# Last two token tiles of a linear-attention and feed-forward kernel: matmul order of the plain products, and which engine makes three of the row sums

## The chip, the core and the metric

The kernel runs on one core of one Trainium2 chip. The metric is the device time of one execution in microseconds (us). In the text, TensorE (PE in the profile) does the matmuls, VectorE (DVE) and ScalarE (ACT) the elementwise work, GpSimd (POOL) some elementwise work and the weight loads, SyncE (SP) issues most transfers. A name with a q behind it (SPq, ACTq) is an engine's queue issuing a transfer.

## The reference

```python
# q, k, v: (8 batches, 8 heads, 576 positions, 64); w_in: (512, 2048); w_out: (2048, 512)
q_s = softmax(q, axis=-1)                 # over the 64 features
k_s = softmax(k, axis=2)                  # over the 576 positions
kv  = einsum('bhsd,bhse->bhde', k_s, v)
x   = einsum('bhsd,bhde->bhse', q_s, kv)  # then laid out as (4608 tokens, 512)
h   = x @ w_in
out = maximum(0.01 * h, h) @ w_out        # float32, (4608, 512)
```

## The kernel before

The 4608 tokens are nine tiles of 512. Attention fills `xT` (features on the partitions, bfloat16) batch by batch, and beside it the feed-forward part runs over the tiles: layer 1 writes a 128x512 block of the hidden layer for each of 16 blocks, a leaky ReLU (line 572) takes it out of PSUM, layer 2 (line 584) sums over the 16 blocks. Every engine runs its instructions in the order in which the kernel's text issues them; there is no scheduler behind it. What an engine waits for is put in as semaphore waits.

The last two tiles, number 7 (`TA`, here called tile A) and number 8 (`TB`, tile B), are done otherwise: both layers use a scheme with seven products in place of eight, in which sums of operands are multiplied and the results are added up.

In layer 1 the operands are the two tiles. `pair_layer1(i)` runs for i = 0 to 7 and gives four hidden blocks each time: of tile A, `g7[i]` and `g7[8+i]`, and of tile B, `g8(i)` and `g8(8+i)`. The additions out of PSUM are VectorE's (line 1027), the leaky ReLUs ScalarE's (line 572). The last leaky of tile A, of `u4` into `g7[15]`, is held back to the end.

In layer 2 each tile is cut by token rows into two halves of 256 (h = 0, 1), by the hidden dimension into two halves of 8 blocks (fh = 0, 1), and by output columns into two halves of 256. Written h0(0) for rows half 0, hidden half 0, and so on, a tile needs these operands:

- plain: h0(0) and h0(1), straight from the hidden blocks (products p1, p2)
- row sums, in a 4-byte format for the fast fp32 matmul: r1 = h1(0) + h1(1), r2 = r1 - h0(0), r3 = h0(0) - h1(0), r4 = h0(1) - r2, and c22, a copy of h1(1)
- weight sums v1 to v4 and o22, made long before

A product is `product2`, 16 matmuls of 256 columns: for each of two groups of 128 rows (i), the 8 hidden blocks (m) are summed in PSUM. p5 = r1 v1, p6 = r2 v2, p7 = r3 v3, p4 = c22 v4, p3 = r4 o22. p1, p2, p5, p6, p7 have both row groups in one PSUM bank; p4 and p3 take a bank for each group. There are six such banks, and a product takes the one whose last reader stands earliest in the order; it waits for that reader, an addition.

The order written out at the end of the kernel is, for TensorE: p1 of A, p1 of B, p2 of A, p2 of B, then p5, p6, p7, p4, p3 of A, then p5, p6, p7, p4, p3 of B. For VectorE after the last pair: r2 of A; the output additions of p2 of A (`second`); r4 of A; `second` of B; r1 of B; u2 and u4 (`sixth`); r2 of B; u3 and two output additions (`seventh`); r3 of B; the additions of p4 and p3 (`fourth`, `third`); r4 of B; then `sixth`, `seventh`, `fourth`, `third` of B. The row sums of A are made in parts of 2, 4 and 2 blocks (the blocks lie in different buffers), those of B in two parts of 4 blocks (128x1024).

r1 and r3 of A are made ahead: `sums_ahead(n)`, n = 0 to 3, makes parts of two blocks (128x512) on GpSimd while the pairs run, n = 3 after the last pair. r2 of A is written over nothing, but r1, r2, r3, r4, c22 of B reuse the buffers of A's (r1 of B has one of its own, that of an earlier weight sum), so a sum of B waits for the product of A that reads the same buffer.

Three waits matter later and stand in the built program both before and after the change, beside those for operands: p5 of B takes the bank of p7 of A and so waits for u3 of A on VectorE; r3 of B waits for the last matmul of p7 of A, whose operand it overwrites; p3 of B waits for r4 of B.

An output row group goes out as two transfers (`put`), for tile A both from SyncE's queue, for tile B one from SyncE's and one from ScalarE's.

Of the kernel before, what the change touches and what calls it, by code (L numbers as in the profile page):

```python
# [12 lines left out]
ALU = mybir.AluOpType  # L13
# [13 lines left out]
def kernel(  # L27
# [9 lines left out]
    nc = tc.nc  # L37
# [10 lines left out]
    P = 128  # L48
# [730 lines left out]
    NH = NF // 2  # L779
    CL, CR = slice(0, 2), slice(2, 4)  # L780
    XA, XB = slice(TA * TT, TB * TT), slice(TB * TT, NT * TT)
    late = {}
# [194 lines left out]
    def g7_blocks(h):  # L977
        ts = lambda t: slice(t * TT + h * M2, t * TT + (h + 1) * M2)
        return (
            (slice(0, 2), lambda fh: g7_pairs[fh][:, :, ts(0)]),  # L980
            (slice(2, 4), lambda fh: xT[:, 0:2, ts(4 + fh)]),
            (slice(4, 6), lambda fh: xT[:, 2:4, ts(4 + fh)]),
            (slice(6, 8), lambda fh: xT[:, 2 * fh : 2 * fh + 2, ts(6)]),
        )
# [6 lines left out]
    def g8_wide(h):  # L991
        ts = lambda t: slice(t * TT + h * M2, t * TT + (h + 1) * M2)
        return tuple((slice(4 * b, 4 * b + 4), lambda fh, b=b: xT[:, :, ts(2 * fh + b)]) for b in range(2))

    def late_rows(name, n, pool):
        late[name] = pool.tile([P, NH, M2], F32R, name=n)

    def sums_ahead(n):
        if n == 0:
            for name in ("r3", "r1"):  # L1000
                late_rows(name, name, late["ahead"])
        (ms, h0), (_, h1) = g7_blocks(0)[n], g7_blocks(1)[n]
        for name, x, y, op in (("r3", h0(0), h1(0), ALU.subtract), ("r1", h1(0), h1(1), ALU.add)):
            nc.gpsimd.tensor_tensor(out=late[name][:, ms], in0=x, in1=y, op=op)

    def product(w, a):
        ps = psB_pool.tile([P, TT], FP32, name="pp", tag=BANK_TAG)
# [12 lines left out]
    def pair_layer1(i):  # L1020
# [36 lines left out]
        if i in (2, 4, 6):  # L1057
            sums_ahead(i // 2 - 1)
# [15 lines left out]
    held_leaky[0]()  # L1074
    next(fill, None)
    sums_ahead(3)
    pairs.close()
    last_pool = ctx.enter_context(tc.tile_pool(name="late3", bufs=1, reuse_waits="tile"))

    def product2(a, w, each=False):  # L1080
        if each:
            ps = [psB_pool.tile([P, H2], FP32, name="pq", tag=BANK_TAG) for _ in range(2)]
        else:
            both = psB_pool.tile([P, 2, H2], FP32, name="pq", tag=BANK_TAG)
            ps = [both[:, 0], both[:, 1]]
        for i in range(2):
            for m in range(NH):
                nc.tensor.matmul(  # L1088
                    ps[i],
                    lhsT=a(m)[:, i * P : (i + 1) * P],  # L1090
                    rhs=w(m),
                    start=(m == 0 and (each or i == 0)),
                    stop=(m == NH - 1 and (each or i == 1)),
                )
        return ps if each else both

    def add(o, ps, e):
        nc.vector.tensor_tensor(out=o, in0=ps, in1=e, op=ALU.add)

    def row_sums(wide, name, n, pool, op, x, y):  # L1100
        late_rows(name, n, pool)
        for (ms, h0), (_, h1) in zip(wide(0), wide(1)):
            view = lambda s: late[s][:, ms].bitcast(FP32) if isinstance(s, str) else (h0, h1)[s[0]](s[1])
            o = late[name][:, ms]
            if op is None:
                nc.scalar.copy(out=o, in_=view(x))
            else:
                nc.vector.tensor_tensor(out=o, in0=view(x), in1=view(y), op=op)

    rows = lambda n: (lambda m: late[n][:, m])  # L1110
    plain_g = lambda g, fh: (lambda m: g(fh * NH + m)[:, 0:M2])
    plain_w = lambda fh: (lambda m: w_out_sb[:, fh * NH + m, E1])
    last_adds = lambda n: [last_pool.tile([P, O], FP32, name=f"{n}{i}") for i in range(2)]
    gu = lambda: g_pool.tile([P, 2, H2], FP32, name="gu", tag="gj")
    A = dict(t=TA, o1=[osb_pool.tile([P, O], FP32, name="out_sb") for _ in range(2)], issue=(nc.sync, nc.sync))
    B8 = dict(t=TB, o1=last_adds("o1"), issue=(nc.sync, nc.scalar))
# [6 lines left out]
    def first_two(z):  # L1123
        z["e1"] = gu()
        nc.scalar.copy(out=z["e1"], in_=z["p1"])

    def second(z):
        for i in range(2):
            add(z["o1"][i][:, E1], z["p2"][:, i], z["e1"][:, i])
            put(z, z["o1"][i], 0, i, E1)  # L1130
# [11 lines left out]
    def fourth(z):  # L1142
        for i in range(2):
            add(z["o2"][i][:, E1], z["p4"][i], z["u3"][:, i])
            put(z, z["o2"][i], 1, i, slice(0, O))
# [5 lines left out]

    ga, gb = (lambda n: g7[n]), g8
    ahead_pool = late["ahead"]
    A["p1"] = product2(plain_g(ga, 0), plain_w(0))
    first_two(A)
    row_sums(g7_wide, "r2", "r2", last_pool, ALU.subtract, "r1", (0, 0))
    B8["p1"] = product2(plain_g(gb, 0), plain_w(0))
    first_two(B8)
    row_sums(g7_wide, "c22", "c22", last_pool, None, (1, 1), None)
    A["p2"] = product2(plain_g(ga, 1), plain_w(1))  # L1160
    second(A)
    row_sums(g7_wide, "r4", "r4", last_pool, ALU.subtract, (0, 1), "r2")
    B8["p2"] = product2(plain_g(gb, 1), plain_w(1))
    second(B8)
    A["p5"] = product2(rows("r1"), rows("v1"))
    late["r1"] = strip("r1").rearrange("p a b -> p (a b)")[:, 0 : NH * M2].rearrange("p (m t) -> p m t", t=M2)
    for (ms, h0), (_, h1) in zip(g8_wide(0), g8_wide(1)):
        nc.vector.tensor_tensor(out=late["r1"][:, ms], in0=h1(0), in1=h1(1), op=ALU.add)
    A["p6"] = product2(rows("r2"), rows("v2"))
    A["o2"] = [osb_pool.tile([P, O], FP32, name="out_sb") for _ in range(2)]  # L1170
    B8["o2"] = last_adds("o2")
# [4 lines left out]
    A["p4"] = product2(rows("c22"), rows("v4"), True)  # L1176
    row_sums(g8_wide, "c22", "c22", last_pool, None, (1, 1), None)
    A["p3"] = product2(rows("r4"), rows("o22"), True)
    row_sums(g8_wide, "r3", "r3", ahead_pool, ALU.subtract, (0, 0), (1, 0))
    fourth(A)  # L1180
    third(A)
    B8["p5"] = product2(rows("r1"), rows("v1"))
# [40 lines left out]
```

## Time and profile before

| what | value |
|---|---|
| time, median of 3 runs | 281.03 us (281.0 to 281.08) |
| the profiled execution's own time | 280.83 us |
| its span, first to last instruction | 279.0 us |
| granted TensorE clock, mean | 0.998 |
| TensorE matmul busy | 270.0 us, 97% of the span |
| VectorE busy | 229.2 us, 82% |
| ScalarE busy | 166.1 us, 60% |
| GpSimd busy | 84.2 us, 30% |

Rows of the timeline read: start in us, duration in us, engine, line of the kernel, operation, output and inputs, shapes, x count, and in brackets how long the engine was idle before and what ended that. Neighbouring rows of one kind are merged, and their durations overlap a little because the engines pipeline. Rows of the waits read: engine and line that waited, on whom, then us in total, times, and the longest in us. Rows of the groups read: line, engine, operation, shapes, count, busy us, mean ns of one, and idle us before. Line numbers are those of the kernel before.

### The profile page before, as it was taken

The numbers are of one execution on the slowest core, as the hardware profiler recorded it, in microseconds if no ns is written. First come the engines' busy times: TensorE is split into PE (matmuls) and PEld (weight loads), VectorE is DVE, ScalarE is ACT, GpSimd is POOL, SyncE is SP. The second block draws the span as 40 slices with busy tenths as digits, with TensorE's granted clock in tenths as the row PEclk, the third lists the DMA queues.
The fourth block names the chain that finished last, engine by engine and source line by source line (L and its number), as shares of the span: only waits on it lengthen the run. The fifth ranks groups of instructions, "written<-read, shape, count | busy, mean of one in ns | idle before, by whom it ended". The sixth has DMA issues, their size and how long they took to land.

```text
span 279.0 us, 5241 instructions
## 1 busy us (share of the span) xinstructions
PE 270.0 (97%) x2018; PEld 148.7 (53%) x2018; DVE 229.2 (82%) x327; ACT 166.1 (60%) x291; POOL 84.2 (30%) x105
## 2 busy tenths in 40 slices
PE   8799999999999999999999999999999999999992
PEld 3378644444444544445444544444445566569992
DVE  2996986899999949956795598958959999998993
ACT  3977573783488467754586448664673667673200
POOL 2867460159003004000300085003000898822000
PEclk9999999999999999999999999999999999999999
DMA  7999999987996697099409940430701010111134
GB/s 244 330 208 324 242 254 284 395 261 223 261 391 215 95 392 261 2 224 390 133 0 248 396 101 2 85 77 1 161 0 40 0 38 0 41 38 41 36 87 141
DMA packets 40488, 46.48 MB, mean 167 GB/s; under 512 B 18832, under 2 KB 24208, under 8 KB 40464
## 3 DMA queue, kind: packets, MB, share of 16 engines
q1 hardware_dynamic: 36480, 41.43, 49.3%
q0 software_dynamic: 3504, 4.20, 8.6%
q10 hardware_dynamic: 480, 0.52, 0.6%
q8 instruction: 16, 0.26, 0.4%
q14 instruction: 8, 0.07, 0.1%
HBM read 36.70 MB, written 9.44 MB: 165 GB/s over the span
## 4 chain that ended last, share of the span: by engine, by line
PE 88%; DVE 6%; DMA 2%; issue 1%; ACT 0%; SPq 0%; DVEq 0%
PE ph L563 35%; PE pout L584 34%; PE pq L1088 9%; PE pp L1009 7%; DVE u L1027 3%; DMA k_raw<-in_k_dram 2%; PE po L479 2%; DVE t L160 1%; PE pokv L341 1%; PE pkv L341 1%; DVE c L1027 1%; PE pkv L419 0%; DVE k_raw L410 0%; ACT ke L206 0%; ACT xT L572 0%
## 5 line engine op out<-in xcount | busy, mean ns | idle before, releaser
L584 PE MATMUL pout<-w_out_sb,gj 128*128 128x512 bf16 x448 | 103.7, 380 | 0.0
L563 PE MATMUL ph<-xT,w_in_sb 128*128 128x512 bf16 (+1 forms) x512 | 98.7, 352 | 0.0
L563 PEld LDWEIGHTS <-w_in_sb 128*128 128x128 bf16 x512 | 49.8, 98 | 47.0 <-issue 0.2
L572 ACT ACTIVATE gj<-ph 128x512 bf16<-128x512 f32 x112 | 63.4, 602 | 18.8 <-PE ph L563 18.5
L584 PEld LDWEIGHTS <-gj 128*128 128x128 bf16 x448 | 41.9, 98 | 51.9 <-issue 4.6
L218 POOL CAST vb<-v_raw 128x1152 bf16<-128x1152 f32 x13 | 19.6, 1536 | 83.7 <-DMA v_raw<-in_v_dram 43.6
L578 ACT COPY out_sb<-pout 128x512 f32<-128x512 f32 x24 | 14.0, 584 | 34.1 <-PE pout L584 20.3
L321 DVE TENSOR_REDUCE qsum<-qe 128x36 f32<-128x2304 bf16 (+5 forms) x13 | 20.1, 1543 | 6.3 <-ACT qe L312 6.2
L1027 DVE TENSOR_TENSOR u<-pp,u 128x512 f32<-128x512 f32 x32 | 21.3, 687 | 2.0 <-PE pp L1009 0.5
L206 ACT ACTIVATE ke<-k_raw 128x2304 bf16<-128x2304 f32 (+2 forms) x13 | 18.0, 1383 | 8.2 <-DVE k_raw L198 7.8
L328 DVE TENSOR_TENSOR qe<-qe,qrec 128x2304 bf16<-128x2304 bf16 (+5 forms) x13 | 21.5, 1657 | 0.4
L245 DVE TENSOR_REDUCE qmax<-q_raw 128x36 f32<-128x2304 f32 (+5 forms) x13 | 20.0, 1537 | 0.6 <-DMA q_raw<-in_q_dram 0.6
L312 ACT ACTIVATE qe<-q_raw 128x2304 bf16<-128x2304 f32 (+5 forms) x13 | 17.2, 1322 | 4.2 <-POOL q_raw L304 3.2
L198 DVE TENSOR_TENSOR k_raw<-k_raw,kall 128x1152 f32<-128x1152 f32 (+2 forms) x10 | 18.1, 1821 | 0.3
L304 POOL TENSOR_TENSOR q_raw<-q_raw,qmax 128x512 f32<-128x512 f32 (+3 forms) x7 | 11.8, 1681 | 21.0 <-DVE qmax L245 20.7
L1009 PE MATMUL pp<-s,t 128*128 128x512 f32 x48 | 17.0, 458 | 0.0
L160 DVE TENSOR_TENSOR t<-t 128x256 f32<-128x256 f32 (+2 forms) x22 | 14.4, 654 | 0.7
L361 DVE RECIPROCAL krec<-pokv 128x2 f32<-128x2 f32 x8 | 1.3, 165 | 16.6 <-PE pokv L479 16.6
L500 ACT CAST xT<-po 128x448 bf16<-128x448 f32 (+3 forms) x31 | 13.3, 513 | 1.1 <-PE po L479 1.1
L304 DVE TENSOR_TENSOR q_raw<-q_raw,qmax 128x2304 f32<-128x2304 f32 (+1 forms) x6 | 13.2, 2202 | 0.2
L160 DVE TENSOR_TENSOR t<-k_raw 128x512 f32<-128x512 f32 (+1 forms) x11 | 11.2, 1016 | 1.1 <-DMA k_raw<-in_k_dram 1.0
L1088 PE MATMUL pq<-v,r 128*128 128x256 f32 x96 | 11.9, 284 | 0.0
(122 smaller groups left out, 324.9 us busy)
## 6 DMA issues: line engine op xcount, KB each, us to landing
out_dram<-out_sb SPq DMA_DIRECT2D x60, 128.0 KB, 4.2
q_raw<-in_q_dram SPq DMA_DIRECT2D x6, 1152.0 KB, 9.1
v_raw<-in_v_dram SPq DMA_DIRECT2D x6, 1152.0 KB, 11.8
k_raw<-in_k_dram SPq DMA_DIRECT2D x5, 1152.0 KB, 6.9
k_raw<-in_k_dram SPq DMA_DIRECT2D x6, 576.0 KB, 6.4
v_raw<-in_v_dram SPq DMA_DIRECT2D x4, 576.0 KB, 7.9
w_in_sb<-in_moe_w_in_dram POOLq DMA_DIRECT2D x7, 256.0 KB, 7.0
w_out_sb<-in_moe_w_out_dram POOLq DMA_DIRECT2D x6, 256.0 KB, 9.2
```

Source lines behind the costliest of these rows:

```text
L160: nc.vector.tensor_tensor(out=o, in0=i0, in1=i1, op=ALU.max)
L218: eng.tensor_copy(out=o, in_=i)
L245: nc.vector.tensor_reduce(out=o, in_=st[b]["q"][:, hs, rs], axis=AX.X, op=ALU.max)
L304: eng.tensor_tensor(out=qs, in0=qs, in1=st[b]["qmax", rs.start, hs.start].unsqueeze(3).to_broadcast([P, m, n, D]), op=ALU.subtract,)
L321: nc.vector.reduce_sum(out=qsum, in_=q_cols(b, rs, hs), axis=AX.X)
L328: nc.vector.tensor_tensor(out=qes if out is None else out, in0=qes, in1=st[b]["qrec", rs.start, hs.start].unsqueeze(3).to_broadcast([P, n, ...
L563: nc.tensor.matmul(ph, lhsT=w_in_sb[:, cb, j * P : (j + 1) * P], rhs=xT[:, cb, c0 : c0 + n], start=(cb == 0 and first), stop=(cb == NB - 1 ...
L572: nc.scalar.activation(out=o, in_=ph, func=AF.Prelu, alpha=LEAKY_SLOPE)
L584: nc.tensor.matmul(pout, lhsT=g_sb[j // 2][:, j % 2, tsub * P : (tsub + 1) * P], rhs=w_out_sb[:, j, os], start=(j == 0), stop=(j == NF - 1),)
L1009: nc.tensor.matmul(ps, lhsT=w(c), rhs=a(c), start=(c == 0), stop=(c == 1))
L1027: nc.vector.tensor_tensor(out=o, in0=ps, in1=e, op=ALU.add)
L1088: nc.tensor.matmul(ps[i], lhsT=a(m)[:, i * P : (i + 1) * P], rhs=w(m), start=(m == 0 and (each or i == 0)), stop=(m == NH - 1 and (each or ...
```

## The change

Four things change, all in the last two tiles.

1. The four plain products (p1 and p2 of A and of B) go over the hidden blocks outside and the two row groups inside: m = 0 for both groups, then m = 1 for both, up to m = 7. Before, group 0 went over all eight blocks and then group 1.
2. In `sums_ahead` r1 is made before r3, and the last part of r1 (n = 3) is made by VectorE. The other seven parts stay with GpSimd.
3. r1 of tile B is made by GpSimd. Before, VectorE made it.
4. r3 of tile B is made by GpSimd. Before, VectorE made it.

No instruction is added or taken out; VectorE loses four of 128x1024 and gains one of 128x512.

```diff
-        for name, x, y, op in (("r3", h0(0), h1(0), ALU.subtract), ("r1", h1(0), h1(1), ALU.add)):
-            nc.gpsimd.tensor_tensor(out=late[name][:, ms], in0=x, in1=y, op=op)
+        for name, x, y, op in (("r1", h1(0), h1(1), ALU.add), ("r3", h0(0), h1(0), ALU.subtract)):
+            eng = nc.vector if (name, n) == ("r1", 3) else nc.gpsimd
+            eng.tensor_tensor(out=late[name][:, ms], in0=x, in1=y, op=op)
...
-    def product2(a, w, each=False):
+    def product2(a, w, each=False, turns=False):
...
-        for i in range(2):
-            for m in range(NH):
-                nc.tensor.matmul(
+        order = [(i, m) for i in range(2) for m in range(NH)]
+        if turns:
+            order = [(i, m) for m in range(NH) for i in range(2)]
+        for i, m in order:
+            nc.tensor.matmul(
...
-    def row_sums(wide, name, n, pool, op, x, y):
+    def row_sums(wide, name, n, pool, op, x, y, eng=nc.vector):
...
-                nc.vector.tensor_tensor(out=o, in0=view(x), in1=view(y), op=op)
+                eng.tensor_tensor(out=o, in0=view(x), in1=view(y), op=op)
...
-    A["p1"] = product2(plain_g(ga, 0), plain_w(0))
+    A["p1"] = product2(plain_g(ga, 0), plain_w(0), turns=True)
...
-    B8["p1"] = product2(plain_g(gb, 0), plain_w(0))
+    B8["p1"] = product2(plain_g(gb, 0), plain_w(0), turns=True)
...
-    A["p2"] = product2(plain_g(ga, 1), plain_w(1))
+    A["p2"] = product2(plain_g(ga, 1), plain_w(1), turns=True)
...
-    B8["p2"] = product2(plain_g(gb, 1), plain_w(1))
+    B8["p2"] = product2(plain_g(gb, 1), plain_w(1), turns=True)
...
-        nc.vector.tensor_tensor(out=late["r1"][:, ms], in0=h1(0), in1=h1(1), op=ALU.add)
+        nc.gpsimd.tensor_tensor(out=late["r1"][:, ms], in0=h1(0), in1=h1(1), op=ALU.add)
...
-    row_sums(g8_wide, "r3", "r3", ahead_pool, ALU.subtract, (0, 0), (1, 0))
+    row_sums(g8_wide, "r3", "r3", ahead_pool, ALU.subtract, (0, 0), (1, 0), nc.gpsimd)
```

More of the change, by code (lines that the diff above doesn't have):

```diff
@@ L1085, in product2 @@
             ps = [both[:, 0], both[:, 1]]
-        for i in range(2):
-            for m in range(NH):
[L1088 to L1094, printed above, removed]
+        order = [(i, m) for i in range(2) for m in range(NH)]
[3 more added lines that the diff above has]
+            nc.tensor.matmul(
+                ps[i],
+                lhsT=a(m)[:, i * P : (i + 1) * P],
+                rhs=w(m),
+                start=(m == 0 and (each or i == 0)),
+                stop=(m == NH - 1 and (each or i == 1)),
+            )
         return ps if each else both
```

## The prediction

> **What bounds the kernel now.** I read the page first (busy times, then the chain that ended last), and from there only the last 35 us, where every changed instruction runs.
>
> ```profile
> PE 270.0 (97%) x2018; PEld 148.7 (53%) x2018; DVE 229.2 (82%) x327; ACT 166.1 (60%) x291; POOL 84.2 (30%) x105
> PE 88%; DVE 6%; DMA 2%; issue 1%; ACT 0%; SPq 0%; DVEq 0%
> ```
>
> TensorE carries 88% of the chain. Only a hole in its work, or the time behind its last matmul, can move the end. One of the windows of 5 us says how near the next engine is in the stage of the change:
>
> ```profile
> 255.00:260.00 5.00, 5.00 (x44) 5.00 (x44) 4.98 (x7) 0.00 (x0) 0.00 (x0) 1.00 0.46 103
> ```
>
> The columns are sum, PE, PEld, DVE, ACT, POOL, clock, DMA share, GB/s. TensorE and VectorE are both full; GpSimd is empty. Next, TensorE's timeline, with the one row of weight loads whose wait the matmul rows hide:
>
> ```profile
> 246.69 0.38 PE L1088 MATMUL pq<-w_out_sb,gj 128*128 128x256 bf16 x2
> 246.91 0.71 PE L1088 MATMUL pq<-w_out_sb,xT 128*128 128x256 bf16 x5
> 248.10 0.28 PE L1088 MATMUL pq<-w_out_sb,xT 128*128 128x256 bf16 x1 [0.49 <-ACT xT L572]
> ...
> 250.09 0.88 PEld L1088 LDWEIGHTS <-xT 128*128 128x128 bf16 x9 [0.35 <-ACT xT L572]
> ...
> 251.09 0.38 PE L1088 MATMUL pq<-w_out_sb,gj 128*128 128x256 bf16 x2
> ...
> 254.50 6.00 PE L1088 MATMUL pq<-v,r 128*128 128x256 f32 x48
> ...
> 264.18 5.92 PE L1088 MATMUL pq<-v,r 128*128 128x256 f32 x48
> ...
> 271.86 2.08 PE L1088 MATMUL pq<-o,r 128*128 128x256 f32 x16
> ```
>
> There are two holes, both at the eighth hidden block of a p1. From p1 of B on (p2 of A starts at 251.09) TensorE runs without one to 273.94.
>
> **Part 1, the plain products.** A plain matmul comes every 0.11 us (246.69, then two later 246.91). ScalarE delivers the blocks that are waited for, the last two of them in this row:
>
> ```profile
> 249.41 1.23 ACT L572 ACTIVATE xT<-u 128x512 bf16<-128x512 f32 x2 [0.17 <-DVE u L1027]
> ```
>
> Block 7 of A is there by 248.10, where the first hole ends; p1 now wants it as its 15th matmul, at 246.69 + 14 x 0.109 = 248.22, so that wait goes. p1 of B then starts at 248.43 and wants its block 7 at 249.96; it comes with the first of the two u, half way through their row, and its weights load at 250.09. So 0.13 us of the second hole stays, and p2 of A starts at 250.31 in place of 251.09: **0.78 us gained**. The held block (250.64) is wanted by p2 of A only at 251.84. Alternating between row groups itself I cost at nothing: the same matmuls and weight loads.
>
> If nothing else waited, A's p5, p6, p7, p4, p3 would start at 253.72, 255.72, 257.64, 259.56, 261.48, and p5 of B at 263.40.
>
> **Parts 2 to 4, the sums.** These are the rows of GpSimd and VectorE that carry the rest.
>
> ```profile
> 226.33 2.28 POOL L1004 TENSOR_TENSOR r<-gj 128x512 fp32r<-128x512 bf16 x2
> ...
> 248.13 1.16 POOL L1004 TENSOR_TENSOR r<-xT 128x512 fp32r<-128x512 bf16 x1 [5.25 <-ACT xT L572]
> 250.72 2.01 POOL L1004 TENSOR_TENSOR r<-xT 128x512 fp32r<-128x512 bf16 x1 [1.44 <-ACT xT L572]
> ```
>
> ```profile
> 250.49 1.22 DVE L1108 TENSOR_TENSOR r<-r,xT 128x1024 fp32r<-128x1024 f32 x1
> 252.75 0.69 DVE L1108 TENSOR_TENSOR r<-r,xT 128x512 fp32r<-128x512 f32 x1 [1.05 <-POOL r L1004]
> ...
> 257.03 2.35 DVE L1168 TENSOR_TENSOR r<-xT 128x1024 fp32r<-128x1024 bf16 x2
> 259.30 1.41 DVE L1098 TENSOR_TENSOR gu<-pq,gu 128x512 f32<-128x512 f32 x2
> 260.63 2.35 DVE L1108 TENSOR_TENSOR r<-r,xT 128x1024 fp32r<-128x1024 f32 x2
> 262.89 0.69 DVE L1098 TENSOR_TENSOR gu<-pq,gu 128x512 f32<-128x512 f32 x1
> ```
>
> The second GpSimd sum took 2.01 us, not 1.16. VectorE was in a sum with both inputs in SBUF until 251.71, and 251.71 + 1.16 = 252.87 against the recorded end of 252.73: GpSimd stood still until VectorE was through, less 0.14 us of overlap. Does it hold the other way, and who is next when both want to go?
>
> ```profile
> 86.99 1.15 POOL L218 CAST vb<-v_raw 128x1152 bf16<-128x1152 f32 x1 [17.18 <-PE ph L563]
> ...
> 159.94 2.56 DVE L304 TENSOR_TENSOR q_raw<-q_raw,qmax 128x2304 f32<-128x2304 f32 x1
> ...
> 161.52 4.06 POOL L218 CAST vb<-v_raw 128x1152 bf16<-128x1152 f32 x2 [24.17 <-DMA v_raw<-in_v_dram]
> ...
> 162.41 2.16 DVE L160 TENSOR_TENSOR t<-k_raw 128x1024 f32<-128x1024 f32 x1
> ```
>
> VectorE's L304 ends at 162.50. Its next instruction stands right behind and takes 2.16 us in place of the 1.22 of a sum of that size (250.49); two casts of 1.15 fill GpSimd from 161.52 to 165.58. In turns the sum is 162.50 + 1.15 (cast) + 1.22 (VectorE) + 1.15 (cast) - 3 x 0.14 = 165.60. So they alternate, whole instructions, and the one that waited longer goes first. VectorE's additions out of PSUM are free of this: the pair of GpSimd sums at 226.33, under such additions, took 1.14 each.
>
> The price of a 128x1024 sum on GpSimd isn't in the trace. Two of 128x512 take 2.28, the upper end. VectorE's own sums grow from 0.69 to 1.22 with the doubled size, and 1.16 grown by that ratio is 2.05, the lower end. I take 2.12, in the lower half, since one instruction has one start where the pair has two.
>
> The Trainium skill, GPSIMD Engine Reference, section 3.1 (Elementwise — side-by-side cycle accounting), measures a two-input addition of 2048 elements at 4497 ns on GpSimd, about twice VectorE's; half of it, an estimate of 2.25 us for 1024, would add 0.13 us to each of the two sums that count below and make the end 0.3 us later.
>
> Making r1 before r3 in the earlier parts costs nothing: the same two sums back to back (226.33), long before p5 at 253.7. Now the ends, one after the other, each waiting sum ending its own duration less 0.14 after the one before it:
>
> - GpSimd's last r3 part of A runs as before, to 249.29. r1 of B, part 1, finds its inputs long ready: 249.25 to 251.37.
> - VectorE's new r1 part (inputs at 250.64) waits for it: 251.37 + 0.69 - 0.14 = 251.92. The removed wait of 1.05 us before 252.75 is replaced by this one.
> - r1 of B, part 2, has waited since 251.3 and is next: 251.92 + 2.12 - 0.14 = 253.9.
> - r2 of A, three parts on VectorE: 254.43, 255.6, 256.2, against 253.44 before. p6 of A wants the last part at 256.44: covered, by 0.25 us.
> - The following work on VectorE is 2.75 us later, and then 2.27 us earlier, since r1 of B (257.03 to 259.30) is gone: u2 at 259.8, r2 of B ready to start at 261.1 (260.63 before).
> - r3 of B may start on GpSimd when p7 of A has read its buffer, 259.7. It finds no sum in its way and runs to 261.92. r2 of B, part 1, waits: 261.92 + 1.22 - 0.14 = 263.0. r3, part 2, is next: 264.98. r2, part 2: 266.06. u3 behind it: 266.68.
>
> u3 of A frees the bank that p5 of B needs. Before, it ended at 263.58 and p5 started at 264.18: the wait was hidden. Now p5 starts at 266.75 in place of 263.40: **a hole of 3.35 us on TensorE**, where 0.78 was gained, so its work ends 2.57 us later, 264.18 to 273.94 moved to 276.51. Nothing of B waits longer: r3 is there at 265, and r4 of B, behind six output additions (2.2 us by the row of six at 272.19, below), starts at about 268.8 and ends by 271.2, wanted at 274.4. SyncE's queue gets the transfers of A's p2 2.75 us later and those of A's p4 and p3 some 0.75 us later (u3's 3.1 less the 2.35 of the r3 that is gone from VectorE); only B's last transfers stand behind them, and those come later still.
>
> **The end.** Here VectorE's time pays back.
>
> ```profile
> 273.31 2.40 SPq L1121 DMA_DIRECT2D out_dram<-o  x4
> 273.31 2.69 ACTq L1121 DMA_DIRECT2D out_dram<-o  x4
> ```
>
> ```profile
> 272.19 2.21 DVE L1098 TENSOR_TENSOR o<-pq,gu 128x256 f32<-128x256 f32 x6
> ```
>
> Before, the last r4 and the additions behind it kept VectorE busy to 274.40, and four transfers stood in a row on each queue, the last issued by 276.00, 3.0 us before the span's end. Now the p4 and p3 additions come as their products end. The last takes 0.4 us (a sixth of 2.21, rounded up) and some 0.1 to notice, behind 276.51, its transfer is issued from 277.0 to 277.55, and the span ends near 280.6. TensorE's end to the span's end is 4.1 us in place of 5.1.
>
> Sum: -0.78 + 3.35 - 1.0 = +1.6 us on a span of 279.0. The profiled execution is 280.83, so 282.4; the median of the runs shown stands 0.2 above it: **282.6**. With the sum on GpSimd at 2.05 to 2.28 us and 0.2 us either way in the tail: 282.0 to 283.3.
>
> **Rivals.**
>
> *VectorE's next sum goes first* when both want to run. Against it is the row at 162.41; for it, that only a few places show the order. Then r1 of B, part 2, comes behind r2 of A, r2 of B still waits for the first part of r3 (261.79) but not for the second, u3 ends at 264.7, the hole is 1.35 us, and the end is 280.6: 0.4 us under today.
>
> *The two engines don't hinder each other here*, or r2 of B gets ahead of r3. Then TensorE runs through to 273.16, and with the shorter tail 279.2: faster by 1.8. Against it is the 2.01 us row. It decides if r2 of B is ready before 259.7 in place of 261.1.
>
> *The clock drops in the hole*, which is slower than my forecast.
>
> ```profile
> 277.00:279.00 2.00, 0.00 (x0) 0.00 (x0) 0.00 (x0) 0.00 (x0) 0.00 (x0) 0.68 0.07 22
> ```
>
> The granted clock over the last 2 us is 0.68; half speed for 64% of it, so from 277.7, 3.8 us behind the last matmul. The hole of 3.35 us is under that, but not by much. At half speed for 3.4 to 6.8 us, 1.7 to 3.4 us are lost: 284.3 to 286.0. The Trainium skill, TensorE: Matmul & The Clock Gate, Part 1, gives a free-running idle window of about 3.4 us; by it a hole under that length keeps the clock.
>
> **How the numbers follow.** Forecast 0.60; VectorE first 0.12; no hindrance 0.12; clock drop 0.10; a hole of a size between 0.06. A measurement here tells about 0.2% (0.56 us) from no change. Faster is the second rival and half of the first: 0.17. Same is the other half and a part of the sizes between: 0.10. Slower: 0.73. The range from 280.5 to 284.4 holds the forecast, the first rival and the near end of the clock drop.
>
> **What would show it.** Right: no hole at 247.6; r1 of B on GpSimd in two parts, the second near 2.6 us long by waiting; r2 of B on VectorE well over its 2.35 us; TensorE idle before p5 of B, put down to u3 (VectorE, L1101 in the new file); few transfers queued at the end. Wrong: p5 of B starting by 264, or VectorE's sums at their old durations beside GpSimd's.

## The result: slower by 1.2%, and the profile after

The changed kernel takes 284.22 us (median of 4 runs, 283.97 to 285.15) against 281.02 us: a ratio of 1.0119, 95% interval 1.0097 to 1.0142. The forecast was 282.6 us. Direction and range held; the size did not: +3.2 us came where +1.6 was forecast. The profiled execution is the slowest of the four, 285.15 us, span 283.3, and has the lowest granted clock (0.987 against 0.991 to 0.993). Its whole last stage stands 0.2 us later than in the profile of before (p1 of A starts at 246.88, before at 246.69), which has nothing to do with the change and is to be taken off when times are compared.

Line numbers in the rows are now those of the kernel that ran: in the changed kernel the products' matmuls are line 1091 (before 1088), the additions out of PSUM 1101 (1098), the row sums 1111 (1108), the transfers 1124 (1121).

The waits from 244 us on, those of TensorE (PE) and of what feeds it:

```profile
PEld pq L1091 <- issue: 3.5, 1, 3.5
PE pq L1091 <- DVE gu L1101: 3.3, 1, 3.3
DVE gu L1101 <- PE pq L1091: 2.7, 2, 2.2
...
PEld L1091 <- ACT xT L572: 0.2, 1, 0.2
```

TensorE's two waits for ScalarE in p1 are down to the 0.2 of the weight load, as wanted. A new one of 3.3 us stands in front of a product (`pq`), and what ended it is a VectorE addition (`gu`, line 1101): u3 of A. The same stage in TensorE's timeline:

```profile
253.93 6.00 PE L1091 MATMUL pq<-v,r 128*128 128x256 f32 x48
259.76 2.08 PE L1091 MATMUL pq<-v,c 128*128 128x256 f32 x16
261.68 2.08 PE L1091 MATMUL pq<-o,r 128*128 128x256 f32 x16
267.11 8.36 PE L1091 MATMUL pq<-v,r 128*128 128x256 f32 x48 [3.35 <-DVE gu L1101]
275.31 2.08 PE L1091 MATMUL pq<-v,c 128*128 128x256 f32 x16
277.23 2.08 PE L1091 MATMUL pq<-o,r 128*128 128x256 f32 x16
```

Two things are to be seen. The hole before p5 of B. And the row behind it: the same 48 matmuls that took 5.92 us before take 8.36 us now. The sums on GpSimd and VectorE:

```profile
249.43 4.67 POOL L1171 TENSOR_TENSOR r<-xT 128x1024 fp32r<-128x1024 bf16 x2
260.07 5.20 POOL L1111 TENSOR_TENSOR r<-xT 128x1024 fp32r<-128x1024 bf16 x2 [5.98 <-PE pq L1091]
```

```profile
250.86 1.25 DVE L1005 TENSOR_TENSOR r<-xT 128x512 fp32r<-128x512 bf16 x1 [0.70 <-ACT xT L572]
252.03 2.61 DVE L1111 TENSOR_TENSOR r<-r,gj 128x512 fp32r<-128x512 f32 x1
...
261.29 5.07 DVE L1111 TENSOR_TENSOR r<-r,xT 128x1024 fp32r<-128x1024 f32 x2
266.29 0.68 DVE L1101 TENSOR_TENSOR gu<-pq,gu 128x512 f32<-128x512 f32 x1
```

VectorE's r2 of B takes 5.07 us; before, it took 2.35. The first part of r2 of A, a sum of 0.68, takes 2.61: it stands behind one whole GpSimd sum. The windows of the hole:

```profile
262.00:264.00 2.00, 1.76 (x15) 1.56 (x13) 2.00 (x2) 1.93 (x2) 2.00 (x2) 1.00 0.05 11
264.00:267.00 3.00, 0.00 (x0) 0.00 (x0) 2.97 (x3) 0.00 (x0) 1.28 (x1) 0.78 0.00 0
267.00:270.00 3.00, 2.89 (x13) 2.92 (x14) 3.00 (x7) 0.00 (x0) 0.00 (x0) 0.50 0.24 53
```

TensorE's granted clock (the column behind the five engines) falls to a half inside the hole: 0.78 over 3 us is half speed for the last 1.3 us, from 265.7, only 1.9 us behind the end of the last matmul (263.76). The window from 270 to 275 has a clock of 0.75, so the half speed lasts to 272.5, 6.8 us in all.

The end of the kernel, where the gain was forecast:

```profile
277.35 2.92 SPq L1124 DMA_DIRECT2D out_dram<-o  x4
277.36 2.95 ACTq L1124 DMA_DIRECT2D out_dram<-o  x4
```

The last transfer is issued by 280.3, 1.0 us behind TensorE's end (279.31); before it was 2.1 us (276.00 against 273.94).

### The profile page after: what moved, and what is told of

The parts are those of the page before. It is cut to its first block, busy times and chain, and to the rows that moved or that the text cites. A ratio compares the mean times of both kernels' runs of the same rounds, so it can differ in the third digit from the quotient of the medians.

```text
span 283.3 us, 5245 instructions
## 1 busy us (share of the span) xinstructions
PE 273.3 (96%) x2018; PEld 151.6 (54%) x2018; DVE 230.9 (82%) x324; ACT 166.2 (59%) x291; POOL 91.9 (32%) x108
## 4 chain that ended last, share of the span: by engine, by line
PE 85%; DMA 5%; DVE 4%; POOL 2%; issue 1%; SPq 0%; DVEq 0%
PE pout L584 35%; PE ph L563 32%; PE pp L1010 9%; PE pq L1091 6%; DVE r L1111 3%; DMA w_in_sb<-in_moe_w_in_dram 3%; DMA k_raw<-in_k_dram 2%; PE po L479 1%; POOL w_in_sb L133 1%; PE pokv L341 1%; PE pkv L341 1%; DVE gu L1101 0%; DVE o L1101 0%; POOL vb L218 0%; POOL qe L273 0%
## 5 line engine op out<-in xcount | busy, mean ns | idle before, releaser
L1091 PE MATMUL pq<-v,r 128*128 128x256 f32 x96 | 14.4, 319 | 3.3 <-DVE gu L1101 3.3
L1091 PEld LDWEIGHTS pq<-v,r 128*128 128x128 f32 x96 | 14.0, 228 | 3.5 <-issue 3.5
L160 DVE TENSOR_TENSOR t<-t 128x256 f32<-128x256 f32 (+2 forms) x22 | 13.5, 615 | 0.7
```

Of the source, the lines that this page charges most:

```text
L1091: nc.tensor.matmul(ps[i], lhsT=a(m)[:, i * P : (i + 1) * P], rhs=w(m), start=(m == 0 and (each or i == 0)), stop=(m == NH - 1 and (each or ...
```

## The experiments

Theory 1 is the prediction's: VectorE's sums with two inputs in SBUF and GpSimd's sums take turns by whole instructions; r3 of B on GpSimd therefore stretches r2 of B, u3 behind r2 is late, and u3 holds the bank of p5 of B. To it comes, from the trace after, a clock drop in that hole. Each ratio below is to the kernel before on the same chip, with its 95% interval.

### r3 of B back to VectorE

```diff
-row_sums(g8_wide, "r3", "r3", ahead_pool, ALU.subtract, (0, 0), (1, 0), nc.gpsimd)
+row_sums(g8_wide, "r3", "r3", ahead_pool, ALU.subtract, (0, 0), (1, 0))
```

> The changed kernel with r3 of tile B given back to VectorE; r1 of B stays on GpSimd. Theory 1 (r3 of B on GpSimd and r2 of B on VectorE take turns, whole instructions, and u3 behind them holds p5 of B): r2 of B takes its own 2.35 us, u3 ends near 264.3, the hole before p5 of B shrinks from 3.35 to 0.8 us or less, no clock drop. VectorE is then full again at the end, and the time is 281.3 to 281.8. Rival (r1 of B on GpSimd, which makes r2 of A 2.8 us later, is what makes the hole): the hole stays near 3 us and the time near 284.

281.39 us, ratio 1.0016 (1.0006 to 1.0025).

```profile
260.89 2.35 DVE L1111 TENSOR_TENSOR r<-r,xT 128x1024 fp32r<-128x1024 f32 x2
263.16 0.68 DVE L1101 TENSOR_TENSOR gu<-pq,gu 128x512 f32<-128x512 f32 x1
```

r2 is back at 2.35 us, and TensorE's wait for u3 is 0.6 us. So the other three parts of the change together cost 0.4 us, against 3.2 with r3 of B. r1 of B on GpSimd does not free VectorE here: the two sums of r1 of B (2.3 us before) are gone, but the first part of r2 of A again takes 2.61 us behind a GpSimd sum, and the part of r1 of A that VectorE took over takes 1.25. The kernel before with r1 of B on GpSimd and nothing else was not run.

### r1 of B back to VectorE

```diff
-    nc.gpsimd.tensor_tensor(out=late["r1"][:, ms], in0=h1(0), in1=h1(1), op=ALU.add)
+    nc.vector.tensor_tensor(out=late["r1"][:, ms], in0=h1(0), in1=h1(1), op=ALU.add)
```

> The changed kernel with r1 of tile B given back to VectorE; r3 of B stays on GpSimd. Theory 1: r2 of B is ready at about 261, still behind the start of r3 of B on GpSimd (260.1), so the hole before p5 of B stays 3.0 to 3.5 us, the clock drops, and the time is 283.8 to 284.6. Rival (r1 of B on GpSimd is the cause): no hole, 279 to 280.

284.24 us, ratio 1.0102 (1.0065 to 1.0140), three runs from 284.21 to 285.07 and one at 282.40.

```profile
267.18 7.50 PE L1091 MATMUL pq<-v,r 128*128 128x256 f32 x48 [3.26 <-DVE gu L1101]
```

The hole is 3.26 us. The rival is out: with r1 of B where it was before, the loss is the same. The run at 282.40 took the time that the same hole costs at full clock (next experiment); by that and by its mean granted clock (0.996 against 0.987 to 0.992 of the other three) the clock held in its hole. It has no profile.

### TensorE kept busy in the hole

```diff
+fill_ps = psO_pool.tile([P, O], FP32, name="pout", tag="pout")
+for _ in range(28):
+    nc.tensor.matmul(fill_ps[:, 0:H2], lhsT=ident, rhs=w_out_sb[:, 0, E1], start=True, stop=True)
 B8["p5"] = product2(rows("r1"), rows("v1"))
```

> The changed kernel with 28 extra matmuls of 256 columns (identity times a block of weights, into an unused bank, 0.11 us each) on TensorE between p3 of A and p5 of B; nobody reads them. p5 of B starts when it did, 267.1. Theory 1 with the clock drop as the second part of the loss: the clock stays at 1, p5 to p3 of B take 9.8 us in place of 12.2, the time is 282.5 to 282.9. Rival (the rest of the loss isn't the clock): 284 or more.

282.70 us, ratio 1.0055 (1.0039 to 1.0072).

```profile
263.59 3.23 PE L1187 MATMUL pout<-w_out_sb,ident 128*128 128x256 bf16 x28
267.11 5.99 PE L1091 MATMUL pq<-v,r 128*128 128x256 f32 x48 [0.28 <-DVE gu L1101]
```

p5 of B starts at 267.11, as without the extra matmuls, but the 48 matmuls take 5.99 us in place of 8.36, and the granted clock is 1.00 in every window from 244 us on. The kernel is 1.5 us faster by the medians (1.8 by the ratios) with more work: that part of the loss is the clock alone. What is left, 1.7 us over the 280.96 of the same chip (1.5 by the ratio), is the hole less the gain of the plain products and the shorter tail, within 0.1 us of the forecast's +1.6.

### Less of the hole filled

```diff
-for _ in range(28):
+for _ in range(14):   # and 8
```

> The changed kernel with 14 of the extra matmuls (1.5 us) before p5 of B, so that about 1.8 us of the hole stay. By windows the least busy one is 47 to 73% busy: few runs or none drop, median 282.5 to 282.9. If any hole of over 1.5 us drops the clock: 284.

> The changed kernel with 8 of the extra matmuls (0.9 us) in place of 28 before p5 of B, so that about 2.5 us of the hole stay. p5 of B starts when it did. If the clock is judged window by window of about 3.4 us and drops in one that is less than about half busy (43% busy dropped it, 73% did not), most runs have a window with 27 to 60% and drop for one window: 282.5 without, 284.2 with a drop, median 283.5 to 284.3. If a drop needs a hole of 3.3 us: 282.5 to 282.8 throughout.

The row of p5, p6 and p7 of B, with 14 and with 8 extra matmuls:

```profile
267.25 5.99 PE L1091 MATMUL pq<-v,r 128*128 128x256 f32 x48 [1.81 <-DVE gu L1101]
```

```profile
267.01 7.49 PE L1091 MATMUL pq<-v,r 128*128 128x256 f32 x48 [2.45 <-DVE gu L1101]
```

With 14 matmuls a hole of 1.81 us stays: 282.77 us, ratio 1.0080 (1.0055 to 1.0106), three runs at 282.42 to 282.85 and one at 284.19. With 8 a hole of 2.45 us stays: 284.07 us, ratio 1.0117 (1.0104 to 1.0131), all four runs at 283.98 to 284.44. The windows of the profiled execution with 8:

```profile
265.00:270.00 5.00, 2.99 (x17) 3.02 (x18) 4.97 (x9) 0.00 (x0) 0.18 (x1) 0.79 0.17 38
270.00:275.00 5.00, 5.00 (x39) 5.00 (x38) 3.09 (x5) 0.00 (x0) 0.00 (x0) 0.87 0.55 122
```

A clock of 0.79 and 0.87 is half speed for 3.4 us in all, from 267.9 to 271.3: it began when the matmuls already ran again. So no hole of 3.3 us is needed; 2.45 us did it in the profile, and by their times in all four runs; 1.81 us did it in one of four, by its time alone (that run has no profile). Nor does one of 3.3 us do it every time, by the run at 282.40 above. The length of the hole makes a drop more or less likely; it does not decide it alone. That the drop is judged in fixed windows, wherever the hole falls in them, fits this and the lengths of 6.8 and 3.4 us, but is not shown by itself.

### r2 of B as one instruction

```diff
-row_sums(g8_wide, "r2", "r2", last_pool, ALU.subtract, "r1", (0, 0))
+late_rows("r2", "r2", last_pool)     # one 128x2048 sum over both parts
+nc.vector.tensor_tensor(
+    out=late["r2"].rearrange("p (b m) t -> p b m t", b=2),
+    in0=late["r1"].bitcast(FP32).rearrange("p (b m) t -> p b m t", b=2),
+    in1=xT[:, :, 0 : 2 * TT].rearrange("p m (b t) -> p b m t", b=2)[:, :, :, 0:M2],
+    op=ALU.subtract)
```

> The changed kernel with r2 of tile B as one VectorE instruction of 128x2048 in place of two of 128x1024. Theory 1: it waits for the first part of r3 only (to about 262.1), runs 2.3 us, u3 ends near 265, the hole is 1.2 to 1.6 us, r3's second part runs behind it; if the clock holds the time is 280.4 to 281.0. Rival (the engines slow each other all the time rather than by whole instructions): r2 takes 5 us as before and the time stays near 284.

280.60 us, ratio 0.9992 (0.9976 to 1.0009). The profiled execution took 282.69 us: its granted clock was 0.66 from 10 to 20 us, and everything behind stands 2 us later. In the last stage the clock is 1.00:

```profile
262.10 6.29 POOL L1111 TENSOR_TENSOR r<-xT 128x1024 fp32r<-128x1024 bf16 x2 [5.98 <-PE pq L1091]
...
263.32 3.08 DVE L1178 TENSOR_TENSOR r<-r,xT 128x2048 fp32r<-128x2048 f32 x1
```

```profile
267.15 5.98 PE L1091 MATMUL pq<-v,r 128*128 128x256 f32 x48 [1.36 <-DVE gu L1101]
```

This is the rule of turns seen directly: with the same number of elements in one instruction, GpSimd gets one turn less before r2 is through. r2 takes 3.08 us in place of 5.07, GpSimd's r3 6.29 in place of 5.20, and the hole is 1.36 us. That more than halves the hole, and the clock holds: 3.6 us for merging two instructions.

### One part of the change at a time

The new order of the plain products, alone on the kernel before:

```diff
-A["p1"] = product2(plain_g(ga, 0), plain_w(0))
+A["p1"] = product2(plain_g(ga, 0), plain_w(0), turns=True)   # and the other three
```

> The kernel before with the new order of the plain products alone; all sums where they were. Theory 1: p2 of A starts 0.78 us earlier and TensorE's last matmul ends up to 0.7 us earlier (p5 of B waits for u3, so it can't gain all), but VectorE is full from r2 of A on and ends its last addition at 274.4 as before, so the time is 280.8 to 281.1, no change. Rival (TensorE alone sets the end): 280.2 to 280.3.

280.82 us, ratio 1.0002 (0.9993 to 1.0011): no change. TensorE's matmuls do end earlier (273.30, with the shift below taken off 0.45 us before the 273.94 of the kernel before), but VectorE's last row starts at 272.00, against 272.19 before in a profile whose last stage stands at 246.50 in place of 246.69: the same time.

```profile
271.22 2.08 PE L1090 MATMUL pq<-o,r 128*128 128x256 f32 x16
```

```profile
272.00 2.08 DVE L1100 TENSOR_TENSOR o<-pq,gu 128x256 f32<-128x256 f32 x6
```

The last part of r1 on VectorE, alone on the kernel before:

```diff
-for name, x, y, op in (("r3", ...), ("r1", ...)):
-    nc.gpsimd.tensor_tensor(...)
+for name, x, y, op in (("r1", ...), ("r3", ...)):
+    eng = nc.vector if (name, n) == ("r1", 3) else nc.gpsimd
+    eng.tensor_tensor(...)
```

> The kernel before with one part of the change alone: r1 before r3 in the sums made ahead, and the last part of r1 on VectorE. Theory 1: the part starts at 250.7 when its block comes, r2 of A ends 0.3 us later than before, and VectorE, full from there on, ends 0.3 us later: 0.2 to 0.4 us slower than before (0.1%). Rival (it saves the 1.05 us wait of r2 for GpSimd): up to 1 us faster.

281.14 us, ratio 1.0009 (1.0000 to 1.0018), +0.28 us. As by theory 1, at the edge of what can be told from nothing.

r3 of B on GpSimd, alone on the kernel before:

```diff
-row_sums(g8_wide, "r3", "r3", ahead_pool, ALU.subtract, (0, 0), (1, 0))
+late_rows("r3", "r3", ahead_pool)
+for (ms, h0), (_, h1) in zip(g8_wide(0), g8_wide(1)):
+    nc.gpsimd.tensor_tensor(out=late["r3"][:, ms], in0=h0(0), in1=h1(0), op=ALU.subtract)
```

> The kernel before with one part of the change alone: r3 of tile B on GpSimd. Theory 1: r3 starts when p7 of A ends (260.6), within 0.05 us of r2 of B on VectorE. Where r3 goes first, r2's two parts wait for one part of r3 each, u3 ends near 267, p5 of B has a hole of about 3 us, and the clock drops: 283.5 to 285. Where r2 goes first, the hole is about 1.4 us: 280.5 to 281.2. Rival (r3 on GpSimd does harm only together with r1 of B there): no hole, 279.5 to 280.5.

281.27 us, ratio 1.0013 (1.0003 to 1.0022), 0.07 us above the range for r2 first.

```profile
260.48 4.30 DVE L1108 TENSOR_TENSOR r<-r,xT 128x1024 fp32r<-128x1024 f32 x2
```

```profile
260.50 6.28 POOL L1181 TENSOR_TENSOR r<-xT 128x1024 fp32r<-128x1024 bf16 x2 [7.92 <-PE pq L1088]
```

VectorE came first by 0.02 us. r2 then stands behind one GpSimd part, not two, and TensorE's wait is 1.25 us, without a clock drop. So r3 alone is enough for a hole. That its size hangs on which engine is first follows from the turns: in the changed kernel GpSimd was first, by 1.2 us (260.07 against 261.29), and the hole was 3.35. This kernel was not run with GpSimd first.

The old order of the plain products in the changed kernel (`turns=True` taken out four times):

> The changed kernel with the old order of the plain products; the three sums stay where the change put them. Theory 1: p7 of A ends 0.8 us later, so r3 of B starts 0.8 us later and u3 too; the hole before p5 of B stays at 3.2 to 3.5 us and all behind it is 0.8 us later: 284.6 to 285.4, with the clock drop of the changed kernel. Rival (VectorE alone sets u3, whatever TensorE does): the hole is 2.5 us, the time as the changed kernel's or less.

284.52 us, ratio 1.0126 (1.0102 to 1.0151), runs from 283.16 to 284.96: a little under the expected range.

```profile
254.34 6.00 PE L1091 MATMUL pq<-v,r 128*128 128x256 f32 x48
...
262.10 2.08 PE L1091 MATMUL pq<-o,r 128*128 128x256 f32 x16
267.52 7.47 PE L1091 MATMUL pq<-v,r 128*128 128x256 f32 x48 [3.35 <-DVE gu L1101]
```

From p5 of A to p5 of B it is 13.18 us, as in the changed kernel (253.93 to 267.11): r3 starts with the end of p7, so an earlier TensorE moves the whole tangle and leaves the hole as it is. The hole stayed at 3.35, as theory 1 said, and the rival's 2.5 is out. In the profiled execution the clock took one stretch of half speed of 3.4 us (7.47 us for the 48 matmuls), where the changed kernel's has 6.8 us (8.36). Why the median fell short of the range is not shown: with four runs each it moves with how much clock each run lost, and the run at 283.16 has, going by its time and its mean clock (0.997 against 0.992 and 0.993), lost none in the hole.

### A way out: u3 first, and r3's second part behind r2

```diff
-row_sums(g8_wide, "r2", "r2", last_pool, ALU.subtract, "r1", (0, 0))
 seventh(A)
+row_sums(g8_wide, "r2", "r2", last_pool, ALU.subtract, "r1", (0, 0))
```

> The changed kernel with u3 and the two output additions of A (seventh) put before r2 of B on VectorE. Theory 1: u3 ends near 262, so p5 of B starts at 263.6 without a hole; r2 of B then still waits for r3's second part (until 264.2), ends near 266.5, and p6 of B has a hole of about 0.5 us; no clock drop; 279.5 to 279.9. Rival (the sums on GpSimd cost the same wherever they stand): 282 or more.

280.44 us, ratio 0.9992 (0.9983 to 1.0001). The hole is gone from p5 and 0.40 us stand before p6, as expected, but the time is 0.5 us over the range. Then, besides, the second part of r3 waits on GpSimd:

```diff
+    if n == 1:   # between the two parts of r3 of B
+        nc.gpsimd.tensor_copy(out=gate, in_=late["r2"][:, NH - 1, 0:1].bitcast(FP32))
     nc.gpsimd.tensor_tensor(out=late["r3"][:, ms], in0=h0(0), in1=h1(0), op=ALU.subtract)
```

> The same as the kernel with u3 first, and the second part of r3 of B on GpSimd is held until r2 of B has ended (a copy of one element of r2 stands before it). Theory 1: r2 runs 262.7 to 265.0 at its own durations, r3's second part 265.2 to 267.4, just ahead of its use at 267.9; no hole at all; 279.0 to 279.4. Rival (p7 of B then waits for r3): 279.6 or more.

279.81 us, ratio 0.9971 (0.9961 to 0.9981): the only version that beats both kernels, by 0.3%, and again 0.4 us over the expected range. TensorE runs without a hole, and yet:

```profile
262.38 2.35 DVE L1111 TENSOR_TENSOR r<-r,xT 128x1024 fp32r<-128x1024 f32 x2
...
264.94 2.14 POOL L1186 TENSOR_TENSOR r<-xT 128x1024 fp32r<-128x1024 bf16 x1
...
265.98 3.31 DVE L1111 TENSOR_TENSOR r<-xT,r 128x1024 fp32r<-128x1024 bf16 x2
...
271.00 2.08 PE L1091 MATMUL pq<-o,r 128*128 128x256 f32 x16
271.25 2.29 DVE L1101 TENSOR_TENSOR o<-pq,gu 128x256 f32<-128x256 f32 x6
272.37 2.40 SPq L1124 DMA_DIRECT2D out_dram<-o  x4
272.37 2.69 ACTq L1124 DMA_DIRECT2D out_dram<-o  x4
```

r2 runs at its own 2.35 us, but now r4 (265.98) stands behind r3's second part and takes 3.31. VectorE ends at 273.54, 0.5 us behind TensorE, and the last four transfers again stand in a row on each queue, to 275.06, as before. From TensorE's end to the span's end it is 5.1 us, as before, and with u3 first alone it is 4.9: the tail's 1.0 us, which I had counted, is all but not won. That is most of the miss in both expectations.

## Why the prediction was right in kind and half in size

The step that failed is the clock drop, which the sum left out and held for a rival with a chance of 0.10. The rest of the sum came out as worked out. That the time, with the drop in it, still lies inside the stated range, at 284.22 of 284.4, is owed to the range's upper end, which took in the near end of that rival; it lies outside the 282.0 to 283.3 worked out for the sum alone. Point by point, by its steps:

- **Plain products, 0.78 us gained on TensorE.** Right: p5 of A to p1 of A is 253.93 - 246.88 = 7.05 us, before 254.50 - 246.69 = 7.81; a gain of 0.76. That alternating the row groups costs nothing held as well. Alone it moves nothing, since VectorE ends where it ended.
- **GpSimd's price of a 128x1024 sum, 2.12 us taken from two bounds.** A free one stands in the row at 264.94 above: 2.14. The estimate from the Trainium skill, GPSIMD Engine Reference, section 3.1, 2.25, was 5% high here; the page's inputs are float32, these are bfloat16.
- **Turns by whole instructions.** Right, link by link: r2 of B was to start at 261.1 and end at 266.06; it starts at 261.29 and ends at 266.36, 0.2 of it the shift of the whole profile. The one-instruction r2 shows the turns by themselves.
- **The hole, 3.35 us.** Measured 3.35 between the matmul records. Shown to come from r3 on GpSimd (r3 given back to VectorE: 0.6) and not from r1 (r1 given back: 3.26).
- **The tail, 1.0 us won.** Right: the last issue ends 1.0 us behind TensorE in place of 2.1.
- **The sum without a clock drop, +1.6 us.** The kernel with the hole filled measures +1.7.
- **The clock drop, held for a rival with a chance of 0.10 and 1.7 to 3.4 us.** This is the step that failed. Its size in the median is 1.5 us (284.22 against 282.70 filled), 2.4 in the profiled execution (8.36 against 5.92). I had read, from the end of the trace, that the clock drops 3.8 us behind the last matmul, and took this for the length of idle that it needs. It was one reading of something that varies: at the ends of other traces the drop comes between 2.3 us (the last part of r1 alone) and 4.0 us (the new order alone) behind the last matmul, and in the changed kernel's hole it came at 1.9. In the partly filled holes a drop came in one run of four at 1.81 us and in four of four at 2.45. The Trainium skill, TensorE: Matmul & The Clock Gate, Part 1, has the drop after at least one idle window of about 3.4 us; I drew on it for that a shorter hole keeps the clock. The runs here differ from it: holes of 3.26 and 2.45 us lost the clock, and, going by the time of one run in four, so can one of 1.81 us. The measurement decides. A hole of 3.35 us should have carried the clock drop as the likely case: the 282.6 of the sum and the 1.5 us measured for the drop make 284.1.

## What to carry to other kernels

A sum moved to GpSimd, though that engine is idle, can cost the engine that it relieves: if the other's neighbouring instructions read two SBUF operands, each of them stands behind a whole GpSimd instruction. So find what VectorE does in the stretch, and put GpSimd's sums beside its work out of PSUM, or make the VectorE side one large instruction.

A hole in TensorE's work has two prices: its length, and, here in one run of four at 1.8 us and in most from 2.45 us on, a time at half clock, 1.5 us in the median. Ask for every new wait whether it is that long.

When one engine's hole is closed, read which engine ends last before counting the gain: the new matmul order won 0.76 us on TensorE and nothing in time, and the best version is again bound by VectorE.

## What the runs showed of the hardware that I had not expected

In the changed kernel's profile TensorE's granted clock fell to a half 1.9 us after its last matmul, with 1.4 us of the hole still to come, and stayed there for 6.8 us though matmuls ran again from 267.11 on. In the three other profiles with a drop in the hole it fell only when matmuls ran again, and for 3.4 us: 3.3 us behind the last matmul in front of a hole of 2.45 us, 3.6 us behind it with holes of 3.26 (r1 of B on VectorE) and 3.35 us (old order). So nearly the same hole can cost one stretch or two. A hole of 1.36 us left the clock at full speed in the profiled execution, and so did one of 1.81 us in its own.

A lead of 0.02 us (VectorE at 260.48, GpSimd at 260.50) was enough for VectorE to stand behind one GpSimd instruction. Where GpSimd led, in the changed kernel, it stood behind two, and the hole was 3.35 us in place of 1.25. These are two kernels: that the lead alone made the difference is argued from the turns, not shown.
